# Attention with a gated bilinear block on one core: denominators of the last quad by a selection product, the last output product kept in PSUM, gate logits as rows, x in two loads

## The chip, the cores and the metric

The kernel runs on one core of one Trainium2 chip. The metric is the device time of an execution in microseconds (us), smaller is better. "Span" is the profiled execution from its first to its last instruction; it is about 2 us shorter than the time of the same run (728.7 against 730.78 for the kernel before). Ratios are the mean time of one kernel's runs over that of the other's of the same rounds, so they are not quite the ratios of the medians quoted beside them.

The engines: TensorE (PE, with its weight loads as PEld), VectorE (DVE), ScalarE (ACT), GpSimd (POOL), SyncE (SP, here only issuing DMAs).

## The reference

```
x = A_x                                             # 1 x 2048 x 512, bf16
g = sigmoid((x * gate_w).sum(-1))                   # one gate per row
a = attention(x, wqkv, wo)                          # 32 heads of 16, softmax over 2048 keys
b = ((x @ w_gate) * (x @ w_up)) @ w_down            # hidden width 1376
out = g * a + (1 - g) * b
```

## The kernel before

The whole program is planned while it is built: a list scheduler in the kernel file steps five clocks (one per engine) with fixed guesses of each duration and so decides the order of the instructions on each engine. The chip then runs that fixed order. Any edit of one part changes the order of everything after it.

The attention is done in 32 "quads" of heads, each for 512 queries: scores (TensorE), exponentials, PV products (TensorE, into one PSUM bank `psO`), normalisation. Three quarters of the exponentials run on ScalarE, in groups of two or three 512-wide tiles; the rest is made on VectorE and GpSimd by integer arithmetic. Everything else that TensorE has to do (q, k, v, gate, up, down and output projections) is a list of "fills", each with a wanted position counted in ScalarE tiles, put between score runs in that order. A "pack" is four matmuls on four column groups of the array; the chain of the kernel before lists 0.21 to 0.22 us for four.

The parts that the change touches (cuts marked by `# ...`):

```python
# four loads of x, alternating between two queues; wk before wq
for t in range(4):
    d_xs.append(load("sp" if t % 2 == 0 else "act", xs[:, t, :], x2[t * 128 : (t + 1) * 128, :], ...))
d_wk[0] = load("act", wk[:, :, 0:128], ...)
d_wq[0] = load("act", wq[:, :, 0:128], ...)

# f_gate: 16 packs of 4 one-column matmuls, full 128x128 weight loads of xT
for kt in range(KD):
    r = e.matmul(bk.ap[:, t : t + 1], xT[:, kt, t * 128 : (t + 1) * 128], gw[:, kt : kt + 1], ...)

# do_pv: in the last quad, each PV matmul is followed by one with "ones" weights,
# which sums the denominators, broadcast over 32 rows, into the bank DB
if lastq:
    for j, kt, k, cell, s0, s1 in specs:
        r = e.matmul(DB.ap[32 * j : 32 * j + 32, :], ones[:, k, :], cell_ap(cell, 1), ...)

# f_wo, last 512 queries: a fill of 4 packs (the fourth with zero-padded weights woz[0],
# for the half of the heads that is ready), evacuated by VectorE into a partial sum;
# at the very end the other half (woz[1]) and a second VectorE combine.
for tt in range(4):
    a1 = act: oraw = Ln(DB)         # denominators
    a2 = act: rb = Exp(-oraw)       # reciprocals
    mt = dve: OX = psO * rb
    pe:  tailb[tt] = OX.T @ woz[1]  # start=True, stop=True
    # then dve: out = gate * tailb + partial sum, and the store
```

The last four combines, one for each 128 rows, are the program's last VectorE work.

The softmax here doesn't subtract the row's maximum and nothing guards it: scores larger than these inputs give would overflow.

## Time and profile before

| | us |
|---|---|
| time, median of the runs made before the change was known | 731.68 (730.24 to 734.92) |
| head: start to first exponential | 10.70 |
| middle: first exponential to end of the last | 705.02 |
| tail: from there to the end | 13.01 |

The three stages are read from the timeline of ScalarE. The page of the kernel before: busy time by engine (section 1), two of the rows of 40 slices (section 2), and the chain that ended last (section 4).

```profile
span 728.7 us, 21767 instructions
PE 695.8 (95%) x9207; PEld 193.3 (27%) x9207; DVE 635.8 (87%) x1196; ACT 704.2 (97%) x687; POOL 420.0 (58%) x443
...
ACT  4999999999999999999999999999999999999993
PEclk9999997999999999999999999999999999999999
...
ACT 87%; PE 10%; DVE 2%; DMA 1%; issue 0%; ACTq 0%; DVEq 0%
```

ScalarE is busy for 97% of the span and is 87% of the chain: the middle is exponentials back to back. So the middle can only shrink where ScalarE waits. The clock row shows one slice at 7 tenths, near 110 us.

Who ScalarE waited for (waits view of the kernel before; us in total, times, longest):

```profile
ACT oraw L1734 <- PE psS L1139: 5.6, 1, 5.6
ACT KE L550 <- PE psS L521: 4.9, 1, 4.9
...
ACT hT L1565 <- PE psS L455: 2.4, 4, 1.0
ACT wv L1565 <- PE psS L455: 1.5, 3, 0.9
ACT PT L1565 <- PE psS L455: 0.5, 2, 0.2
ACT wd L1565 <- PE psS L455: 0.5, 1, 0.5
```

5.6 us is the wait between the last exponential and the first Ln, at the end; 4.9 is the head; the rest, some 5 us, lies in the middle.

The gate's stretch in windows of 2 us of the kernel before (columns: busy us and instruction count of each engine, granted TensorE clock, DMA):

```profile
104.00:106.00 2.00, 1.36 (x26) 0.82 (x26) 2.00 (x6) 2.00 (x3) 0.53 (x1) 1.00 0.00 0
106.00:108.00 2.00, 1.45 (x26) 0.82 (x26) 2.00 (x5) 2.00 (x2) 1.04 (x1) 0.91 0.00 0
108.00:110.00 2.00, 1.70 (x14) 0.39 (x11) 1.33 (x3) 2.00 (x3) 1.88 (x2) 0.50 0.00 0
110.00:112.00 2.00, 2.00 (x22) 0.50 (x19) 1.21 (x2) 1.64 (x3) 1.18 (x2) 0.50 0.02 4
112.00:114.00 2.00, 2.00 (x26) 0.78 (x26) 1.52 (x3) 1.75 (x2) 1.04 (x1) 0.50 0.04 8
114.00:116.00 2.00, 2.00 (x19) 0.24 (x17) 1.27 (x3) 1.59 (x3) 1.72 (x2) 0.50 0.04 4
116.00:118.00 2.00, 2.00 (x23) 0.37 (x15) 0.61 (x3) 1.52 (x2) 0.33 (x1) 0.53 0.00 0
```

While the gate's one-column matmuls run (from 104.2), TensorE reads 1.36 and 1.45 of 2 us busy; then the clock is 0.50 from 107.6 for 10.24 us, and ScalarE drops to about 1.6 of 2 us.

The chain of the head of the kernel before:

```profile
2.12 5.40 DMA wq<-in_A_wqkv_dram
...
7.66 1.94 PE psS L521 x32
...
9.61 0.61 ACT KE L550
```

wq, the fourth load on its queue, lands at 7.52, and the first product waits for it.

### The profile page before, as it was taken

To read this page: it belongs to the slowest core of one execution; us is meant where nothing else is said; L and a number is where in the kernel's file an instruction comes from. 1 tells how busy PE (TensorE), PEld (TensorE's weight loads), DVE (VectorE), ACT (ScalarE), POOL (GpSimd) and SP (SyncE) were. 2 spreads that over 40 slices of the span, in tenths; PEclk is the share of its full clock that TensorE was granted. 3 is DMA by queue.
4 is the path that set the end of the run, shared out by engine and by line. 5 is a ranking of instruction groups with operands and counts; after the bars stand their busy time and mean duration, and the time that the engine had idled before them with its cause. 6 is when DMAs were issued, how large, how long until landed. Compare 5 with 4: busy or idle time off the path is not lost.

```text
span 728.7 us, 21767 instructions
## 1 busy us (share of the span) xinstructions
PE 695.8 (95%) x9207; PEld 193.3 (27%) x9207; DVE 635.8 (87%) x1196; ACT 704.2 (97%) x687; POOL 420.0 (58%) x443
## 2 busy tenths in 40 slices
PE   7999999999999999999999999989999999999996
PEld 3323332222222222222222222222222222222222
DVE  5888997988989799999988989889888999988886
ACT  4999999999999999999999999999999999999993
POOL 2777665664655666655567665556544655554451
PEclk9999997999999999999999999999999999999999
DMA  7700000000200001000000010000000110000000
GB/s 139 250 3 17 20 17 18 21 16 7 95 20 17 18 14 40 18 18 21 17 18 12 24 42 18 18 8 14 21 17 16 36 32 6 17 20 17 20 18 30
DMA packets 31014, 21.65 MB, mean 30 GB/s; under 512 B 18344, under 2 KB 25928, under 8 KB 30920
## 3 DMA queue, kind: packets, MB, share of 16 engines
q1 hardware_dynamic: 29048, 19.49, 8.9%
q8 instruction: 73, 1.20, 0.7%
q10 hardware_dynamic: 1872, 0.79, 0.5%
q14 instruction: 21, 0.17, 0.1%
HBM read 15.11 MB, written 2.35 MB: 24 GB/s over the span
## 4 chain that ended last, share of the span: by engine, by line
ACT 87%; PE 10%; DVE 2%; DMA 1%; issue 0%; ACTq 0%; DVEq 0%
ACT PT L1565 63%; ACT wv L1565 15%; ACT wd L1565 5%; ACT hT L1565 4%; PE psS L455 3%; PE psO L1128 3%; PE psX L521 2%; DMA wq<-in_A_wqkv_dram 1%; PE psS L521 1%; DVE PT L1005 1%; PE psS L605 0%; PE psX L605 0%; DVE wk L823 0%; PE psX L455 0%; PE psS L1139 0%
## 5 line engine op out<-in xcount | busy, mean ns | idle before, releaser
L1565 ACT ACTIVATE PT<-psS 128x1024 bf16<-128x1024 f32 (+1 forms) x474 | 540.8, 1385 | 0.8 <-PE psS L455 0.5
L1064 POOL TENSOR_SCALAR PT<-PT 128x1024 int16<-128x1024 int16 x320 | 330.7, 1043 | 254.3 <-DVE PT L1061 143.0
L1005 DVE TENSOR_SCALAR PT<-psS 128x512 int16<-128x512 f32 x429 | 290.8, 685 | 41.1 <-PE psS L455 36.3
L455 PE MATMUL psS<-QM,KE 32*128 32x512 bf16 x1968 | 264.7, 379 | 19.4 <-ACT PT L1565 8.2
L1128 PE MATMUL psO<-PT,VS 128*18 128x512 bf16 x1605 | 226.6, 384 | 0.4 <-DVE oraw L1168 0.3
L1128 PE MATMUL psO<-PT,VD 128*18 128x512 bf16 x1400 | 207.9, 383 | 0.1
L1061 DVE TENSOR_SCALAR PT<-PT 128x1024 int16<-128x1024 int16 x375 | 157.7, 456 | 8.3 <-PE psO L1128 5.7
L1565 ACT ACTIVATE wv<-psS 128x1024 bf16<-128x1024 f32 (+1 forms) x120 | 153.1, 1304 | 1.5 <-PE psS L455 1.5
L947 PEld LDWEIGHTS <-KE 32*128 32x128 bf16 x2048 | 63.3, 91 | 275.0 <-issue 273.7
L1128 PEld LDWEIGHTS psO<-PT,VS 128*18 128x18 bf16 x1605 | 53.2, 88 | 58.6 <-issue 36.2
L1005 DVE TENSOR_SCALAR PT<-psX 128x512 int16<-128x512 f32 x77 | 53.0, 688 | 16.8 <-PE psS L455 16.4
L1128 PE MATMUL psO<-wv,VS 128*18 128x512 bf16 x258 | 66.6, 384 | 0.5 <-DVE oraw L1168 0.5
L1128 PEld LDWEIGHTS psO<-PT,VD 128*18 128x18 bf16 x1400 | 48.6, 88 | 45.6 <-issue 31.2
L521 PE MATMUL psX<-xT,wu 128*32 128x512 bf16 x688 | 55.5, 388 | 0.2 <-DVE QM L582 0.2
L521 PE MATMUL psX<-wd,hT 128*32 128x512 bf16 (+1 forms) x704 | 55.7, 384 | 0.0
L521 PE MATMUL psX<-xT,wg 128*32 128x512 bf16 x688 | 53.8, 384 | 0.3 <-DVE usb L726 0.3
L1565 ACT ACTIVATE hT<-psS 128x1024 bf16<-128x1024 f32 (+1 forms) x42 | 45.9, 1246 | 2.4 <-PE psS L455 2.4
L1565 ACT ACTIVATE wd<-psS 128x1024 bf16<-128x1024 f32 (+1 forms) x39 | 46.1, 1260 | 0.6 <-PE psS L455 0.5
L1064 POOL TENSOR_SCALAR wd<-PT 128x1024 int16<-128x1024 int16 x27 | 28.0, 1043 | 8.7 <-PE psO L1128 3.3
L455 PE MATMUL psX<-QM,KE 32*128 32x512 bf16 x80 | 30.2, 378 | 2.3 <-ACT KE L550 0.7
L726 DVE CAST usb<-psX 128x512 bf16<-128x512 f32 (+1 forms) x44 | 30.0, 682 | 2.3 <-PE psX L521 1.8
L758 DVE TENSOR_TENSOR hT<-psX,usb 128x512 bf16<-128x512 f32 (+1 forms) x44 | 30.0, 681 | 2.2 <-PE psX L521 2.0
(89 smaller groups left out, 468.5 us busy)
## 6 DMA issues: line engine op xcount, KB each, us to landing
rb<-rscr SPq DMA_DIRECT2D x31, 256.0 KB
out_dram<-ost SPq DMA_DIRECT2D x12, 128.0 KB, 2.1
wu<-in_B_w_up_dram SPq DMA_DIRECT2D x1, 1376.0 KB, 9.0
wg<-in_B_w_gate_dram SPq DMA_DIRECT2D x1, 1376.0 KB, 12.1
wd<-in_B_w_down_dram SPq DMA_DIRECT2D x1, 1280.0 KB, 6.1
OT<-OX SPq DMA_DIRECT2D x60, 16.0 KB, 1.8
wo<-in_A_wo_dram SPq DMA_DIRECT2D x1, 512.0 KB, 12.4
out_dram<-wk SPq DMA_DIRECT2D x4, 128.0 KB, 1.7
```

What stands on the lines that cost most here:

```text
L455: return e.add_instruction(mybir.InstMatmult(name=nc.get_next_instruction_name(), engine=mybir.EngineType.PE, ins=[e.lower_ap(rhs), e.lowe ...
L521: return e.matmul(out_ap[32 * q : 32 * q + w, :], lhs[:, 32 * q : 32 * q + w], rhs, start=s0, stop=s1, tile_position=(0, 32 * q), skip_gro ...
L726: lambda v: v.tensor_copy(usb[0:w, n % 2, :], bk.ap[0:w, :]),
L758: lambda v: v.tensor_tensor(hT[0:w, f, :], bk.ap[0:w, :], usb[0:w, n % 2, :], ALU.mult),
L947: r = e.ldweights(w, tile_position=pos)
L1005: lambda v: v.tensor_scalar(cell_ap(pr["cell"] + i, 1, mybir.dt.int16), bk.ap, CB, 0.0, ALU.add, ALU.max),
L1061: fn = lambda v: v.tensor_single_scalar(cell_ap(c, n, I16), cell_ap(pr["cell"], n, I16), 32.0 * k, ALU.add)
L1064: fn = lambda g: g.tensor_scalar(cell_ap(c, n, I16), cell_ap(pr["cell"], n, I16), 32.0 * k, 1.0, ALU.add, ALU.mult)
L1128: r = e.matmul(psO[32 * j : 32 * j + VW, :], pv_stationary(m, kt, j, k), cell_ap(cell, 1), start=s0, stop=s1, tile_position=(0, 32 * j), s ...
L1565: lambda a: a.activation(cell_ap(c, n), src, ACT.Exp, scale=LN2 / 128.0),
```

## The change

Intent: take TensorE work out of the end (denominators from `psO` itself, whose rows 16 of each 32 already hold them; the output projections after the PV packs; the last product added in PSUM, so that one VectorE combine for each 128 rows does), make the gate cheap, and start earlier. The core of the diff:

```diff
-        for t in range(4):
-            d_xs.append(load("sp" if t % 2 == 0 else "act", xs[:, t, :], ...))
+        for h in range(2):
+            r_ = load("act" if h else "sp", xs[:, 2 * h : 2 * h + 2, :], ...)
-        d_wk[0] = load("act", ...)      # wk before wq
+        d_wq[0] = load("act", ...)      # wq before wk
...
-            # gate: 64 matmuls of one column, psX <- xT (weights), gw
+                    return e.matmul(bk.ap[32 * q : 32 * q + 1, :], gw[:, kt : kt + 1],
+                                    xT[:, kt, q * 512 : (q + 1) * 512], ...)
+            packs = [... for kt in range(KD)]            # 4 packs; logits as 4 rows of 512
+            # then: copy to SBUF, DMA to memory, DMA back as 128 x 16, exp, 1/(1+.)
...
         # do_pv, last quad
-                if lastq:
-                    ... 112 "ones" matmuls into DB
...
         # f_wo, last 512 queries: 3 packs, result stays in its bank, no evacuation;
         # kept in a list of its own (wts), started only when no PV pack is ready
...
         # filler: hold a fill back when a score run is due; the fourth block's q and k earlier
-            (200.0, 280.0, [("q", 3, 0)] + ...
+            (190, 260, [("q", 3, 0)] + ...
+                    if st["ua"] >= 96 and late < FBL and t + FB * PACK > run_at() and any(AQ):
+                        cand = []
...
         # tail
+            hs.append(dve: hi = bf16(psO[:, cs]))
+            ls.append(dve: lo = psO[:, cs] - hi)
+            pe: dbs[tt][:, cs] = sel.T @ hi ; += sel.T @ lo     # 128-column packs
             a1 = act: Ln(dbs[tt])  ...
-            pe: tailb[tt] = OX.T @ woz[1]              # start, stop
+            pe: tailb[tt] += OT.T @ woz[0] (half) ; += OX.T @ woz[1]
```

Both programs put 1536 tiles of 512 through ScalarE, in 675 and 676 instructions.

More of the change, by code (lines that the diff above doesn't have):

```diff
@@ L229, in _build @@
     out2 = out.rearrange("b s d -> (b s) d")
+    gscr = nc.dram_tensor("gscr", [4, 512], F32, kind="Internal").ap()
     scr = nc.dram_tensor("rscr", [NO, 4, 512], F32, kind="Internal").ap()
@@ L261, in _build @@
         mask = sb("mask", [128, 2], F32)
-        ones = sb("ones", [128, 4, 32], BF16)
+        sel = sb("sel", [128, 128], BF16)
         gex = sb("gex", [128, T], F32)
@@ L319, in _build @@
         d_xs = []
-        for t in range(4):
-            d_xs.append(load("sp" if t % 2 == 0 else "act", xs[:, t, :], x2[t * 128 : (t + 1) * 128, :], f"dxs{t}", 0.5, 2.8))
+        for h in range(2):
+            r_ = load(
+                "act" if h else "sp",
+                xs[:, 2 * h : 2 * h + 2, :],
+                x2[h * 256 : h * 256 + 256, :].rearrange("(t p) d -> p t d", p=128),
+                f"dxs{h}",
+                0.5,
+                3.3,
+            )
+            d_xs += [r_, r_]
         d_wk, d_wq, d_wv = [None] * NB, [None] * NB, [None] * NB
-        d_wk[0] = load("act", wk[:, :, 0:128], wcol(D, D + 128), "dwk0", 0.5, 3.0)
-        d_wq[0] = load("act", wq[:, :, 0:128], wcol(0, 128), "dwq0", 0.5, 3.4)
+        d_wq[0] = load("act", wq[:, :, 0:128], wcol(0, 128), "dwq0", 0.5, 3.6)
+        d_wk[0] = load("act", wk[:, :, 0:128], wcol(D, D + 128), "dwk0", 0.5, 3.6)
         d_wv[0] = load("act", wv[:, :, 0:256], wcol(2 * D, 2 * D + 256), "dwv0", 0.5, 5.0)
@@ L373, in _build @@
         o_vone = o_one
-        for k in range(4):
-            o_one = now("pool", [o_one], lambda g, k=k: g.memset(ones[:, k, :], WK[k]), 0.2)
+        o_sel = now("pool", [], lambda g: g.memset(sel[:], 0.0), 0.3)
+        o_sel = now(
+            "pool",
+            [o_sel],
+            lambda g: g.affine_select(
+                out=sel.rearrange("p (a b) -> p a b", b=32),
+                in_=sel.rearrange("p (a b) -> p a b", b=32),
+                compare_op=ALU.not_equal,
+                fill=1.0,
+                base=-16,
+                pattern=[[-32, 4], [0, 32]],
+                channel_multiplier=1,
+            ),
+            0.4,
+        )
         slots = [
@@ L667, in f_gate, with mk, fn @@
         def f_gate(pos):
-            packs = []
-            for t in range(T):
-                def mk(bk, t=t):
-                    def fn(e):
-                        r = None
-                        for kt in range(KD):
-                            r = e.matmul(
-                                bk.ap[:, t : t + 1],
-                                xT[:, kt, t * 128 : (t + 1) * 128],
-                                gw[:, kt : kt + 1],
-                                start=(kt == 0),
-                                stop=(kt == KD - 1),
-                                skip_group_check=True,
-                            )
-                        return r
-                    return fn
-                packs.append((mk, 0.25, "f"))
+            def mk(bk, kt):
+                def fn(e, q):
+                    return e.matmul(
+                        bk.ap[32 * q : 32 * q + 1, :],
+                        gw[:, kt : kt + 1],
+                        xT[:, kt, q * 512 : (q + 1) * 512],
+                        start=(kt == 0),
+                        stop=(kt == KD - 1),
+                        tile_position=(0, 32 * q),
+                        skip_group_check=True,
+                    )
+                return pack4(fn)
@@ L689, in evac @@
+            packs = [(lambda bk, kt=kt: mk(bk, kt), PACK, "c") for kt in range(KD)]
+            grow = ost.rearrange("p a b -> p (a b)").bitcast(F32)
             def evac(bk, last):
                 bk.need += 1
+                e0 = None
+                e0 = add("dve", [last], lambda v: v.tensor_copy(grow, bk.ap), 0.61, prio=3, cb=lambda k: bk.readers.append(k))
                 e1 = add(
-                    "act",
-                    [last],
-                    lambda a: a.activation(gex[:], bk.ap[:, 0:T], ACT.Exp, scale=-1.0),
@@ L695, in evac @@
-                    0.1,
-                    lat=0.33,
-                    cb=lambda k: bk.readers.append(k),
-                )
-                e2 = add("dve", [e1], lambda v: v.tensor_single_scalar(gden[:], gex[:], 1.0, ALU.add), 0.1)
-                e3 = add("dve", [e2], lambda v: v.reciprocal(gval[:], gden[:]), 0.1)
-                ogate["g"] = add("dve", [e3], lambda v: v.tensor_scalar(omg[:], gval[:], -1.0, 1.0, ALU.mult, ALU.add), 0.1)
+                    "sp",
+                    [e0],
@@ new lines, in evac @@
+                    lambda e: e.dma_start(gscr, grow[0:128:32, :]),
+                    0.1,
+                    lat=3.0,
+                    stream="dgl",
+                    dma=True,
+                )
+                gsrc = bass.AP(gscr.tensor, gscr.offset, [[1, 128], [128, T]])
+                e2 = add(
+                    "sp",
+                    [e1],
+                    lambda e: e.dma_start(gex[:, :], gsrc, allow_slow_non_contiguous=True),
+                    0.5,
+                    lat=9.0,
+                    stream="dgl2",
+                    dma=True,
+                )
@@ L703, in f_gate @@
+                e3 = add("act", [e2], lambda a: a.activation(gval[:], gex[:], ACT.Exp, scale=-1.0), 0.1, lat=0.33)
+                e4 = add("dve", [e3], lambda v: v.tensor_single_scalar(gden[:], gval[:], 1.0, ALU.add), 0.1)
+                e5 = add("dve", [e4], lambda v: v.reciprocal(gval[:], gden[:]), 0.1)
+                ogate["g"] = add("dve", [e5], lambda v: v.tensor_scalar(omg[:], gval[:], -1.0, 1.0, ALU.mult, ALU.add), 0.1)
             return Fill("gate", packs, lambda: [d_gw, o_xt[0]] + d_x[1:], evac, pos)
@@ L811, in _build, with combine @@
         otfree = {}
-        ev_part = {}
-        part = xT[:, :, 512:1536].bitcast(F32)
-        def combine(t, bank_ap, last, cb=None, halves=None):
+        def combine(t, bank_ap, last, cb=None):
             c, tt = divmod(t, 4)
-            fin = t >= T - 4 and halves is None
-            o_dst = ost[:, t % 2, :] if t < T - 4 else part[:, tt, :] if not fin else wk[:, tt, :]
-            src = part[:, tt, :] if fin else b_ap(t)
+            o_dst = ost[:, t % 2, :] if t < T - 4 else wk[:, tt, :]
             k = add(
                 "dve",
-                [last, ev_b[c, tt], ogate["g"]] + ([o_out.get(t - 2)] if t < T - 4 else [ev_part[tt]] if fin else [pe["last"]]),
-                lambda v: v.scalar_tensor_tensor(o_dst, bank_ap, gval[:, t : t + 1], src, ALU.mult, ALU.add),
+                [last, ev_b[c, tt], ogate["g"]] + ([o_out.get(t - 2)] if t < T - 4 else []),
+                lambda v: v.scalar_tensor_tensor(o_dst, bank_ap, gval[:, t : t + 1], b_ap(t), ALU.mult, ALU.add),
                 0.67,
@@ L827, in combine @@
             )
-            if t >= T - 4 and not fin:
-                ev_part[tt] = k
-                return
             bfree[t] = k
@@ L844, in f_wo @@
             lastc = c == NCH - 1
+            nb = NB - 1 if lastc else NB
             packs = [
@@ L847, in f_wo @@
                     lambda bk, b=b: col(
-                        bk.ap,
-                        OT[:, (NB * c + b) % NOT, tt * 128 : (tt + 1) * 128],
-                        woz[:, 0, :] if lastc and b == NB - 1 else wo[:, b, :],
-                        b == 0,
-                        b == NB - 1,
+                        bk.ap, OT[:, (NB * c + b) % NOT, tt * 128 : (tt + 1) * 128], wo[:, b, :], b == 0, b == NB - 1
                     ),
@@ L856, in f_wo @@
                 )
-                for b in range(NB)
+                for b in range(nb)
             ]
             def evac(bk, last):
+                if lastc:
+                    tailb[tt] = bk
+                    bk.need = 99
+                    return
                 for b in range(NB):
@@ L863, in evac @@
                 bk.need += 1
-                combine(t, bk.ap, last, cb=lambda k: bk.readers.append(k), halves=True if lastc else None)
+                combine(t, bk.ap, last, cb=lambda k: bk.readers.append(k))
             def deps():
                 if lastc:
-                    if any(f.name[0] in "ugkvq" for f in fills):
-                        return [None]
-                    return [d_wo, d_woz[0], ev_b.get((c, tt)), o_mult.get(NM - 2)] + [o_ot.get(NB * c + b) for b in range(NB - 1)]
+                    return [d_wo] + [o_ot.get(NB * c + b) for b in range(NB - 1)]
                 if t >= 2 and t - 2 not in o_out:
@@ L1121, in do_pv @@
                 pv_left[m] -= 1
-            if lastq and specs[0][4]:
-                deps += DB.take(99)
             def fn(e):
@@ L1136, in fn @@
                     )
-                if lastq:
-                    for j, kt, k, cell, s0, s1 in specs:
-                        r = e.matmul(
-                            DB.ap[32 * j : 32 * j + 32, :],
-                            ones[:, k, :],
-                            cell_ap(cell, 1),
-                            start=s0,
-                            stop=s1,
-                            tile_position=(0, 32 * j),
-                            skip_group_check=True,
-                        )
                 return r
-            kk = pe_run(deps, fn, PACK * (2 if lastq else 1), "c", t)
+            kk = pe_run(deps, fn, PACK, "c", t)
             for j, kt, k, cell, s0, s1 in specs:
@@ L1231, in _build @@
         fills = [q0[3], q0[0], q0[4], q0[5], q0[1], q0[6], q0[7], q0[2]] + q0[8:]
+        wts = []
+        GP = 200.0
+        K3L = 190
+        K3H = 260
         B1, B2L, B2, B3L, B3 = 40.0, 100.0, 180.0, 200.0, 270.0
@@ L1235, in _build @@
             (90.0, 184.0, [("q", 2, 0), ("k", 2, 0), ("v", 1, 0), ("v", 1, 1), ("k", 2, 1), ("v", 1, 2), ("v", 1, 3), ("k", 2, 2), ("v", 1, 4), ("v", 1, 5), ("k", 2, 3), ("v", 1, 6), ("v", 1, 7)]),
-            (200.0, 280.0, [("q", 3, 0)] + [("k", 3, ch) for ch in range(4)]),
+            (K3L, K3H, [("q", 3, 0)] + [("k", 3, ch) for ch in range(4)]),
         ):
@@ L1240, in _build @@
                 fills.append(f_q(0, b, pos) if kind == "q" else f_k(b, ch, pos) if kind == "k" else f_v(b, ch, pos))
-        GP = 200.0
         F0 = 210.0
@@ L1261, in _build @@
             for tt in range(4):
-                fills.append(f_wo(c, tt, max(PER * NQ * (c + 1) + WP, f0 + step * (c + 1) + 4.0) + 9.0 * tt if c < NCH - 1 else NA - WL))
+                (fills if c < NCH - 1 else wts).append(f_wo(c, tt, max(PER * NQ * (c + 1) + WP, f0 + step * (c + 1) + 4.0) + 9.0 * tt if c < NCH - 1 else NA - WL))
         for c in range(NCH - 1):
@@ L1298, in bank_free, with start_fill @@
             return f is not None and f + SEM <= t
-        def start_fill(f, bk):
-            fills.remove(f)
+        def start_fill(f, bk, lst=None):
+            (fills if lst is None else lst).remove(f)
             f.bank = bk
@@ L1359, in _build @@
         XF = -99
+        FB = 2
+        FBL = 15
         def a_idx():
@@ L1464, in pe_step @@
                 na = len(aus)
-                if ua + na > NA - PER:
-                    st["mq"] = True
                 st["lastd"] = dus[-1] if dus else None
@@ L1500, in pe_step, with run_at @@
             return filler(t, can)
+        def run_at():
+            s = slots[st["slot"]]
+            fr = [s[i].free_at() for i in range(2)]
+            if len(exps) < 2 and all(f is not None for f in fr):
+                return max(max(fr) + SEM, act_need() - 0.62 - MG)
+            if not exps:
+                return clock["pe"]
+            t0 = max(clock["act"], exps[0][2].end + SEM)
+            return t0 + 0.052 + 0.4267 * len(exps[0][0]) + 0.21 + SEM
         st["mq"] = False
-        tailb = []
+        tailb = {}
+        tbs = (X, slots[1][2], slots[1][0], slots[1][1])
         def filler(t, can=True):
@@ L1524, in filler @@
                             break
-            if pv is not None and (nfree < NF or st["fill"] is None):
+            fin = not any(AQ) and all(dnext[j] == len(DU[j]) for j in range(4))
+            if fin and pv is None and st["fill"] is None and wts and fready(wts[0], t):
+                for bk in tbs:
+                    if bank_free(bk, t):
+                        start_fill(wts[0], bk, wts)
+                        break
+            if pv is not None and (nfree < NF or st["fill"] is None or fin):
                 do_pv(pv, t)
@@ L1701, in _build @@
                 clock[e] += 0.02
-            if pvst["m"] >= NM and not fills and st["fill"] is None:
+            if pvst["m"] >= NM and not fills:
                 break
@@ L1715, in _build, with tail_step, pe_tail @@
         drain()
-        assert not fills and st["fill"] is None, [f.name for f in fills]
+        assert not fills, [f.name for f in fills]
+        half = []
+        def tail_step(limit):
+            t = clock["pe"]
+            if st["fill"] is None and wts:
+                for bk in tbs:
+                    if bk.need < 99 and bank_free(bk, t):
+                        start_fill(wts[0], bk, wts)
+                        break
+            if st["fill"] is not None:
+                do_fill(t)
+                return True
+            o = o_mult[NM - 2]
+            if len(half) < len(tailb) and max(o.end, d_woz[0].end) + SEM <= max(t, limit - PACK):
+                tt = len(half)
+                rhs = OT[:, (NB * NCH - 1) % NOT, tt * 128 : (tt + 1) * 128]
+                half.append(pe_run([o, d_woz[0]], col(tailb[tt].ap, rhs, woz[:, 0, :], False, False), PACK, "c", t))
+                return True
+            return False
+        def pe_tail(deps, fn, occ, lat):
+            t = ready(_Task("pe", deps, fn, occ))
+            while t > clock["pe"] + 0.1 and tail_step(t):
+                pass
+            return pe_run(deps, fn, occ, "c", clock["pe"], lat=lat)
         c = NCH - 1
-        tailb = [X, slots[1][2], slots[1][0], slots[0][0]]
         lastpv = pvst["last"]
@@ L1722, in _build @@
         free = o_mult[NM - 1 - NO]
+        hi, lo = usb[:, 0, :], usb[:, 1, :]
+        hs, ls, dens = [], [], []
+        for tt in (0, 1, 0, 1, 2, 3, 2, 3):
+            cs = slice(tt * 128, (tt + 1) * 128)
+            if len(hs) <= tt:
+                hs.append(now("dve", [lastpv], lambda v, cs=cs: v.tensor_copy(hi[:, cs], psO[:, cs]), 0.2))
+            else:
+                ls.append(now("dve", [hs[tt]], lambda v, cs=cs: v.tensor_tensor(lo[:, cs], psO[:, cs], hi[:, cs], ALU.subtract), 0.2))
+        dbs = [slots[0][min(tt, 2)] for tt in range(4)]
+        old = [bk.take(99) for bk in slots[0]] + [[]]
+        for tt in range(4):
+            cs = slice(tt * 128, (tt + 1) * 128)
+            pe_tail([hs[tt], o_sel] + old[tt], col(dbs[tt].ap[:, cs], sel, hi[:, cs], True, False), 0.06, 0.3)
+            dens.append(pe_tail([ls[tt]], col(dbs[tt].ap[:, cs], sel, lo[:, cs], False, True), 0.06, 0.3))
+        dens[2] = dens[3]
         oo = []
@@ L1733, in _build @@
             cs = slice(tt * 128, (tt + 1) * 128)
-            a1 = now("act", [lastpv, free], lambda a, cs=cs: a.activation(lnd[:, cs], DB.ap[:, cs], ACT.Ln), 0.29)
+            a1 = now("act", [dens[tt], free], lambda a, tt=tt, cs=cs: a.activation(lnd[:, cs], dbs[tt].ap[:, cs], ACT.Ln), 0.29)
             a2 = now("act", [a1], lambda a, cs=cs: a.activation(rlast[:, cs], lnd[:, cs], ACT.Exp, scale=-1.0), 0.22)
-            if tt == 3:
+            if tt == 2:
                 fin(0)
@@ L1743, in _build, with last_pack @@
             )
-            oo.append(
-                pe_run(
-                    [mt] + tailb[tt].take(99),
-                    col(tailb[tt].ap, OX[:, (NB - 1) % 2, cs], woz[:, 1, :], True, True),
-                    PACK,
-                    "c",
-                    clock["pe"],
-                )
-            )
+            def last_pack(e, tt=tt, cs=cs):
+                return col(tailb[tt].ap, OX[:, (NB - 1) % 2, cs], woz[:, 1, :], False, True)(e)
+            while len(half) <= tt:
+                assert tail_step(1e9)
+            oo.append(pe_tail([mt], last_pack, PACK, 0.44))
         for tt in range(1, 4):
```

## The prediction

> **What bounds the kernel now.** ScalarE (ACT). The page gives it 704.2 of 728.7 us busy; the chain of waits is 87% ACT, nearly all softmax exponentials. The timeline splits the span into a head (first exponential at 10.70 us), a middle of 705.0 us (last exponential ends at 715.72), and a tail of 13.0 us. In the middle ACT idles about 5 us (stretches: 1.9 in 12 to 50, 1.7 in 100 to 120, 1.1 in 480 to 490, 0.2 elsewhere). The built programs both put 1536 tiles of 512 through ACT (675 and 676 instructions), so the middle can only shrink by that idle time.
>
> **Tail (about -4.0 us).** Before, ACT waits 5.6 us (waits view) from its last exponential to the first Ln, because TensorE still has about 9 PV packs, 9 packs of the "ones" denominators (0.22 us each in the chain) and three output projections (0.86 us each) to do. All 112 "ones" matmuls go (28 packs, an estimated 6 us of TensorE, partly before ACT ends), and the projections move behind the PV packs. By the instruction order only 5 PV packs follow the last score, the last needs the last exponential, and no VectorE partial sum (0.75 us each) stands in between. I expect the last PV to end 0.6 to 1.0 us after the last exponential. Added: eight 128x128 VectorE ops (about 0.22 us each, as the present 128x128 product) and eight short selection packs; estimated 1.3 us until the first Ln. So the 5.6 us wait becomes about 2.1. From the first Ln on, the chain is unchanged in kind (Ln, Exp, product, last pack, four 0.67 us combines, 2.1 us store); 7.4 us now from PV end to the end, about 8.2 afterwards. Tail: 13.0 to about 9.0.
>
> **Gate (about -1.5 us).** The gate now uses 64 one-column matmuls with full weight loads, from 104.2 to 118.2. While they run TensorE stalls (busy 1.36 and 1.45 of 2 us), and the granted clock then reads 0.50 for 10.24 us from about 107.7; the ACT gaps of that stretch (0.25, 0.25, 0.41, 0.48) lie in it. [...] The new gate is 4 packs (0.9 us), so I expect this stretch at full clock and its ACT idle gone. The two new gate DMAs are off the critical path. The second throttle (483 to 487, after a schedule dip) may move, vanish or return.
>
> **Head (about -0.8 us).** The critical load is wq, issued fourth on ACT's queue (2.12) and landing at 7.52; it becomes the second, and x needs one issue (0.4 us) fewer per queue. Then the xT copies (done at 6.96) and wk limit. First exponential near 9.9.
>
> **Middle reshuffle.** Fill order and positions change, so ACT idle elsewhere may rise or fall; I allow +0.5 for it. Sum: -0.8 -1.5 -4.0 +0.5, about -5.8.
>
> **Predicted:** 725.8 us, 80% range 722.5 to 729.5. Faster by over 2%: 0.02; within 2%: 0.97; slower: 0.01.
>
> **Right if:** first exponential at 9.5 to 10.3; no 0.5 clock in the stretch with the gate; ACT idle from last exponential to first Ln 1.5 to 2.7 us; last exponential to end 8.5 to 9.7 us.
>
> **Wrong if:** larger x loads land later and delay everything; a less loaded TensorE dips and throttles elsewhere; the new filler rule starves TensorE fills so that weights or gate come late; the selection chain serialises through semaphores and costs over 2 us.

That the new gate would keep the full clock rests on the trace's order of events (TensorE at 1.36 and 1.45 of 2 us, half clock after it) and was the author's estimate.

## The result

| | before | after |
|---|---|---|
| time, median | 731.0 (730.24 to 734.92, 4 runs) | 721.68 (720.47 to 722.06, 4 runs) |
| ratio | | 0.986, 95% interval 0.9828 to 0.9892 |
| span of the profiled run | 728.7 | 719.0 |
| head / middle / tail | 10.70 / 705.02 / 13.01 | 9.43 / 700.67 / 8.88 |

The change is 1.4% faster; that is inside 2%, as forecast, but the time lies below the range of 722.5 to 729.5. The page after, the same lines:

```profile
span 719.0 us, 21551 instructions
PE 686.3 (95%) x9079; PEld 188.6 (26%) x9079; DVE 633.8 (88%) x1209; ACT 702.8 (98%) x688; POOL 411.6 (57%) x433
...
ACT  5999999999999999999999999999999999999996
PEclk9999999999999999999999999999999999999999
...
ACT 95%; PE 3%; DMA 1%; DVE 1%; ACTq 0%; issue 0%; DVEq 0%
```

The clock row has no slice below 9 any more, and the chain is ScalarE for 95%. Where the gate runs now (its matmuls start between 114.3 and 116.0), the windows read:

```profile
114.00:116.00 2.00, 1.93 (x29) 0.45 (x30) 1.85 (x4) 2.00 (x3) 1.04 (x1) 1.00 0.22 71
116.00:118.00 2.00, 2.00 (x33) 0.56 (x31) 2.00 (x5) 2.00 (x3) 1.04 (x1) 1.00 0.18 69
```

ScalarE's waits after:

```profile
ACT KE L572 <- PE psS L543: 3.9, 1, 3.9
...
ACT hT L1598 <- PE psS L477: 2.4, 4, 1.0
ACT oraw L1808 <- PE psS L543: 1.7, 1, 1.7
```

The wait before the first Ln fell from 5.6 to 1.7 us. In the middle no wait is left, apart from 2.4 us (`hT`) in the first 30 us, which both kernels have. The chain of the head after:

```profile
1.80 5.40 DMA wk<-in_A_wqkv_dram
...
7.24 1.08 PE psS L543 x16
...
8.34 0.61 ACT KE L572
```

Now wk is what the first k product waits for; the q product before it is off the chain.

To see where the middle gained, I counted in both traces when n of the 1536 exponential tiles were done (the "curve", after minus before, in us):

```
tiles done       2     205    250    700   1030   1040   1536   end of program
before, us    11.72  106.45 129.41 334.08 484.38 490.23 715.72  728.73
after - before -1.27  -1.37  -3.96  -3.89  -4.19  -5.49  -5.63  -9.77
```

The gain comes in four steps and is flat between them: 1.3 us in the head, 2.6 us between 106 and 129 us (the gate), 1.3 us between 484 and 490 us, and 4.1 us in the tail; about 0.5 is spread over the rest. The trace of before has two throttled stretches before its tail, 107.6 to 117.8 us and 483.1 to 486.5 us, exactly where the two middle steps are. The trace of after has none, but for the last 0.2 us of the program.

### The profile page after: what moved, and what is told of

It is laid out like the page before. It is cut to its first block, busy times and chain, and to the rows that moved or that the text cites. A ratio compares the mean times of both kernels' runs of the same rounds, so it can differ in the third digit from the quotient of the medians.

```text
span 719.0 us, 21551 instructions
## 1 busy us (share of the span) xinstructions
PE 686.3 (95%) x9079; PEld 188.6 (26%) x9079; DVE 633.8 (88%) x1209; ACT 702.8 (98%) x688; POOL 411.6 (57%) x433
## 4 chain that ended last, share of the span: by engine, by line
ACT 95%; PE 3%; DMA 1%; DVE 1%; ACTq 0%; issue 0%; DVEq 0%
ACT PT L1598 69%; ACT wv L1598 16%; ACT hT L1598 5%; ACT wd L1598 4%; PE psS L543 1%; DMA wk<-in_A_wqkv_dram 1%; PE psO L1150 1%; PE psS L477 0%; PE psS L627 0%; PE psX L627 0%; DVE wk L851 0%; PE psX L477 0%; DVE wd L1029 0%; PE psX L543 0%; ACTq L316 0%
## 5 line engine op out<-in xcount | busy, mean ns | idle before, releaser
L1088 POOL TENSOR_SCALAR PT<-PT 128x1024 int16<-128x1024 int16 x312 | 322.2, 1043 | 250.8 <-DVE PT L1085 129.2
L1029 DVE TENSOR_SCALAR PT<-psS 128x512 int16<-128x512 f32 x441 | 300.0, 686 | 47.4 <-PE psS L477 40.6
L1150 PE MATMUL psO<-PT,VS 128*18 128x512 bf16 x1597 | 220.9, 381 | 0.3 <-DVE oraw L1179 0.2
L1150 PE MATMUL psO<-PT,VD 128*18 128x512 bf16 x1400 | 204.5, 381 | 0.2
L1085 DVE TENSOR_SCALAR PT<-PT 128x1024 int16<-128x1024 int16 x380 | 155.8, 450 | 4.6 <-PE psO L1150 1.4
L1150 PE MATMUL psO<-wv,VS 128*18 128x512 bf16 x257 | 63.1, 381 | 0.1
L1598 ACT ACTIVATE hT<-psS 128x1024 bf16<-128x1024 f32 (+1 forms) x49 | 53.4, 1274 | 2.4 <-PE psS L477 2.4
L1029 DVE TENSOR_SCALAR PT<-psX 128x512 int16<-128x512 f32 x63 | 43.4, 688 | 8.6 <-PE psS L477 8.2
L1598 ACT ACTIVATE wd<-psS 128x1024 bf16<-128x1024 f32 (+1 forms) x34 | 42.5, 1340 | 0.0
L1211 POOL TENSOR_TENSOR OT<-oraw,rb 128x512 bf16<-128x512 f32 x16 | 20.4, 1273 | 13.7 <-DVE PT L1085 13.7
```

Of the source, the lines that this page charges most:

```text
L1029: lambda v: v.tensor_scalar(cell_ap(pr["cell"] + i, 1, mybir.dt.int16), bk.ap, CB, 0.0, ALU.add, ALU.max),
L1085: fn = lambda v: v.tensor_single_scalar(cell_ap(c, n, I16), cell_ap(pr["cell"], n, I16), 32.0 * k, ALU.add)
L1088: fn = lambda g: g.tensor_scalar(cell_ap(c, n, I16), cell_ap(pr["cell"], n, I16), 32.0 * k, 1.0, ALU.add, ALU.mult)
L1150: r = e.matmul(psO[32 * j : 32 * j + VW, :], pv_stationary(m, kt, j, k), cell_ap(cell, 1), start=s0, stop=s1, tile_position=(0, 32 * j), s ...
L1211: lambda e: e.tensor_tensor(dst, oraw[:, s, :], rb[:, s, :], ALU.mult),
L1598: lambda a: a.activation(cell_ap(c, n), src, ACT.Exp, scale=LN2 / 128.0),
```

## The experiments

Fourteen kernels were run, each beside the kernel before. The build-time plan makes clean comparisons of totals hard (below), so most verdicts rest on the curve and on single waits in the traces.

### The parts alone

`gate_only`: the kernel before with the gate part of the diff.

> The kernel before with only the gate as rows. Theory 1 ([...] the clock halves for 10.2 us, and ACT starves): no 0.5 clock near 107 us, the curve of exponential tiles against time gains 2.0 to 2.8 us between 100 and 125 us and nothing before; span 726.0 to 727.0. Theory 2 (the throttle of that stretch comes anyway and the gain there was schedule reshuffle): the throttle stays and the gain is under 1 us. The second throttle near 483 is left open: if it goes too, another 1.1.

(The one-column matmuls were thought to bring the half clock. Theory 1 is that they do: in the trace of before the clock is 0.50 for 10.24 us soon after they start.)

Measured: 728.8 us, ratio 0.9949 (0.9907 to 0.9991). There is no throttle near 107 (clock 1.00 in all windows from 104 to 120 us), and against before the curve goes from +1.59 at tile 205 (this execution had a late head, 12.28, with the clock halved from 8.5 to 11.9 us) to -0.85 at tile 265: 2.4 us, as theory 1 said. The throttle near 483 was absent too (another 1.3). But the span was 729.0, not 726 to 727: the head was 1.6 us later and the tail 14.8 instead of 13.0, and 0.7 was lost near 330 us.

`head_only`: the two x loads and wq ahead of wk, and nothing else.

> The kernel before with only the two x loads and wq ahead of wk. First exponential at 9.4 instead of 10.7 if the head's gain is due to the loads alone; throttles and tail as before; span 727.2 to 727.8. If the first exponential stays later than 10, the shorter gate or constants must have helped.

Measured: 730.0 us, 0.9959 (0.9910 to 1.0008); first exponential 9.28, tail 13.05, both throttles (105.4 and 480.9) still there, span 727.1. This is as expected. Over all runs the head is the noisiest piece: with the old loads the first exponential came at 9.92, 10.05, 10.28, 10.47, 10.54, 10.70, 11.80, 12.20 and 12.28 us, with the new ones at 8.75, 8.80, 9.28, 9.43, 9.53 and 9.56. The medians, 10.54 and 9.36, differ by 1.2 us and the two groups don't overlap. Which of the two edits does it was not separated.

`tail_only`: the end part of the diff, with the old gate, the old loads and the old fill rule.

> The kernel before with only the end changed (selection product, last product kept in PSUM, projections after PV). Tail from last exponential to end 8.6 to 9.2 instead of 13.0 us. The list of fills loses four entries, so the positions of later fills change a little: if the second throttle is luck of the schedule it may move or go; the first (gate) throttle must stay. Span 723.5 to 725.

Measured: 735.56 us, 1.0040 (0.9998 to 1.0083). It missed in both terms. The tail was 11.27, not 8.6 to 9.2, because 10 PV packs were still to do at the last exponential. And the middle lost 6.9 us against before (curve from -0.65 to +6.27): a wait at 162.8 (1.1 us), throttles at 440.8 and 464.7 (3.41 and 6.83 us), and waits of ScalarE for cells that late PV packs had not freed. One of them in ScalarE's timeline of this run (the brackets give the idle time before and what ended it):

```profile
468.69 1.02 ACT L1565 ACTIVATE PT<-psS 128x1024 bf16<-128x1024 f32 x1 [2.75 <-PE psO L1131]
```

So the tail's edit alone, in this plan, is no gain. The losses lie far ahead of the tail's instructions, so it is the order of fills that seems to cost here; this is argued and was not isolated.

`after_oldgate`: the kernel after with the gate part of the diff undone.

> The kernel after with the old gate put back. Theory 1: a 0.5 clock stretch returns near 105 us and the curve loses 2.0 to 2.8 us there; span 721 to 722. Theory 2: under 1 us lost, no throttle.

Measured: 726.82 us, 0.9918 (0.9878 to 0.9959), which is 5.1 us over the kernel after (medians of different rounds). The throttle came back, for 17.07 us from 117.7, and relative to after the curve lost 5.1 us between tiles 205 and 280 and another 1.4 by tile 400, with waits of ScalarE at 158.8 and 165.0 where scores came late. The direction is that of theory 1; the loss is larger than expected, and the stretch lasted five steps of 3.41 us here and not three.

`sched_only`: only the fill rule and the earlier fourth block, in the kernel before.

```diff
-            (200.0, 280.0, [("q", 3, 0)] + ...
+            (K3L, K3H, [("q", 3, 0)] + ...      # 190, 260
+                    if st["ua"] >= 96 and late < FBL and t + FB * PACK > run_at() and any(AQ):
+                        cand = []
```

> The kernel before with only the schedule constants: the new rule that holds a fill back when a score run is due, and the fourth block's q and k fills earlier (190 to 260). The alone-run of the tail was slower than before (735.6), so parts interact. Theory A (the constants keep TensorE from dips and backlogs): the second throttle (483) goes, ACT idle away from the gate falls under 0.5 us, gain 1 to 2 us over before; gate throttle and 13 us tail stay. Theory B (the constants are neutral and the loss of the tail-only run was luck of the fill positions): within 1 us of before at the last exponential.

Measured: 741.83 us, 1.0147 (1.0115 to 1.0179). Both theories missed: it is clearly slower. The gate ran later (115.4 to 131.4) and throttled for 17.07 us, and ScalarE waited 12.0 us before the first Ln, with 14 PV packs, 14 ones packs and 11 packs of the down projection still to do.

`after_nosched`: the kernel after without those constants.

> The kernel after without those constants. Theory A: throttles or ACT idle come back in the middle, TensorE has a backlog at the end (tail 10 to 11.5 us), span 722 to 728. Theory B: within 1 us of after, 718 to 720, tail about 8.9.

Measured: 720.65 us, 0.9860 (0.9836 to 0.9884), curve within 0.4 us of after from tile 205 on, no throttle in the middle, tail 8.62. So the constants add nothing measurable to the change (theory B here), though in the kernel before they cost 11 us.

### What in the gate cost 2.6 us

`gate_x7`: the kernel before with the new gate, its packs seven times over, 28 packs or some 5.9 us of TensorE, about as long as the old gate's 64 weight loads of 0.096 us (6.1 us; both are estimates from the traces' 0.21 us a pack and 0.096 us a load). "Active" and "activity" in this and later expectations mean how busy the traces show TensorE: 1.36 and 1.45 of 2 us at the old gate.

```diff
-            packs = [(lambda bk, kt=kt: mk(bk, kt), PACK, "c") for kt in range(KD)]
+            packs = [(lambda bk, kt=kt: mk(bk, kt), PACK, "c") for _ in range(7) for kt in range(KD)]
```

> The kernel before with the new gate, but its four packs done seven times over (28 packs, about 6 us of fully active TensorE, about as long as the 64 one-column matmuls take). Theory 1 (what cost 2.4 us was the halved clock, from low activity): no throttle near 107, the curve keeps most of the gain of the gate-only run (at least 1.5 of 2.4 us between 100 and 125). Theory 2 (what cost was the TensorE time of the old gate): the gain is gone, under 0.8 us, without a throttle.

Measured in the stretch in question: no throttle (clock 1.00 in all windows from 104 to 120 us); the curve gained 2.5 us between tiles 205 and 265 (from -0.41 to -2.87), the whole gain of `gate_only`. The total is another matter: 741.65 us, 1.0148 (1.0122 to 1.0173). ScalarE's waits in this run:

```profile
ACT oraw L1745 <- PE psS L1150: 8.6, 1, 8.6
ACT wd L1576 <- PE psS L456: 8.6, 3, 4.6
```

The second line is three waits, at 153.5, 159.6 and 168.6: the 28 packs held up the queue of fills behind them, and the casts of the last four key chunks ended at 141.9, 153.0, 159.1 and 168.1 instead of 120.8, 137.7, 144.6 and 153.9 in `gate_only`. So the old gate's cost where it stood was the clock, not the time; but TensorE time in fills has its own price, when a deadline lies behind it. The later losses (1.8 us at 362.6, a tail of 17.0) belong to this plan as well.

`gate_spread`: the kernel before with its old gate, the same 64 one-column matmuls, cut into four fills 16 positions apart.

```diff
-            for t in range(T):
+            for t in range(4 * part, 4 * part + 4):
...
-        fills.append(f_gate(GP))
+        fills.append(f_gate(GP, 0))
+        for gp_ in range(1, 4):
+            fills.append(f_gate(GP + 16.0 * gp_, gp_))
```

> The kernel before with its old one-column gate, cut into four fills of four row tiles each, placed 16 positions apart. Same matmuls, same TensorE time, three more small ACT instructions [...]. Theory 1 (dense one-column matmuls [...] halve the clock): no 0.5 stretch between 90 and 150 us, and the curve gains 1.5 to 2.5 us there against before. Rival (their TensorE time is what costs): no gain. The plan of later fills changes too, so the rest of the span is not compared.

Measured: 729.38 us, 0.9995 (0.9968 to 1.0021), the matmuls now between 105.3 and 143.8 us. The first windows of this run:

```profile
104.00:106.00 2.00, 1.91 (x34) 0.79 (x34) 1.63 (x4) 2.00 (x3) 1.58 (x2) 1.00 0.04 8
106.00:108.00 2.00, 1.63 (x22) 0.47 (x19) 2.00 (x5) 2.00 (x4) 0.84 (x1) 1.00 0.00 0
108.00:110.00 2.00, 1.30 (x19) 0.33 (x19) 2.00 (x5) 2.00 (x4) 0.90 (x2) 1.00 0.01 4
110.00:112.00 2.00, 1.97 (x30) 0.51 (x22) 2.00 (x4) 2.00 (x3) 2.00 (x3) 1.00 0.00 0
```

The clock stays at 1.00 although one window has only 1.30 us of TensorE; it is not followed by another like it. The curve gained 2.4 us (from +1.11 to -1.29 between tiles 205 and 250). The same instructions without their crowding cost no throttle (the clock is 1.00 in these windows, against 0.50 for 10.24 us in the kernel before): together with `gate_only`, `after_oldgate` and `gate_x7` that settles the gate's step. The total gained nothing, since this run's head was late (11.80), keys were late again (0.7 at 162.7) and the tail was 13.9.

### The second throttle

In which executions of before it occurs can be judged by the mean clock: one stretch of 10.24 us at half clock takes 0.7% off it, one of 3.41 us another 0.23% (estimates: half of each over the span of 728.7). Of the 28 runs of before in the four sets of rounds, 15 have a clock of 0.992 or more and so had no room for the second stretch beside the gate's (an inference: only the profiled runs list the stretches); their median is 730.0 us. The median of the other 13 is 731.6; these may have had it, or one in the head or at the end, as some profiled runs show. So it is there in at most half of the executions, among them the profiled one.

`dip_x2` and `dip_x3`: the plan of before, unchanged, with the score matmuls of tiles 1012 to 1034 issued two or three times. Each time the bank is written anew. The outputs are right. "Activity" is again TensorE's busy time: 0.85 of 2 us ahead of the throttle in the kernel before.

```diff
+            times = 2 if aus and 1012 <= st["ua"] <= 1034 else 1
             def fn(e):
-                for u, bk in us:
-                    ...
+                for _ in range(times):
+                    for u, bk in us:
+                        ...
```

> The kernel before, same plan, but the score matmuls of the exponential tiles 1012 to 1034 are issued twice (idempotent; about 0.2 us more TensorE work per run in a stretch where TensorE waits for ScalarE). Low activity as the cause: no 0.5 clock near 483, and the curve gains about 1.3 us between tiles 1030 and 1040. Another cause: throttle and loss stay. The gate throttle near 107 stays in both.

> The same with three times (0.4 us more per run). As for twice; if twice is too little activity to hold the clock, this one still should. Risk: scores come up to 0.4 us later and ACT may wait a little, at most 0.1 us each.

Windows of the kernel before:

```profile
480.00:482.00 2.00, 0.85 (x10) 0.28 (x9) 2.00 (x5) 2.00 (x4) 1.41 (x3) 1.00 0.00 0
482.00:484.00 2.00, 1.77 (x22) 0.41 (x19) 1.96 (x5) 2.00 (x3) 1.03 (x2) 0.78 0.04 4
484.00:486.00 2.00, 2.00 (x18) 0.40 (x17) 0.69 (x1) 1.40 (x2) 1.89 (x2) 0.50 0.03 8
```

and of `dip_x2`:

```profile
480.00:482.00 2.00, 1.68 (x20) 0.51 (x13) 1.96 (x4) 2.00 (x3) 1.42 (x2) 1.00 0.00 0
482.00:484.00 2.00, 1.71 (x27) 0.41 (x19) 2.00 (x5) 2.00 (x3) 1.29 (x2) 1.00 0.07 12
484.00:486.00 2.00, 2.00 (x32) 0.43 (x23) 1.25 (x3) 1.70 (x3) 1.52 (x2) 1.00 0.00 0
```

Before, TensorE is busy 0.85 of 2 us in the window ahead of the throttle, with score runs alone; its longest gap there is 0.60 us. With doubled scores it is 1.68, and no throttle follows. With three times TensorE reads 1.76 or more in every window of 2 us between 478 and 486 us, and none follows either (clock 1.00 from 470 to 490). Against before, `dip_x2` gained 0.6 us between tiles 1030 and 1040 and not 1.3: the doubled work itself probably cost the rest, as ScalarE reads 1.70 of 2 us in one window. `dip_x3` lost 1.0 us between tiles 1000 and 1040 (0.9 of it before tile 1030), probably for that reason, without a throttle. Times: 730.04 (0.9988, 0.9956 to 1.0020) and 732.16 (1.0010, 0.9972 to 1.0048), both unclear against before. The absence might still be chance, as at most half of the executions throttle there: of the timed runs of `dip_x2`, two read a clock of 0.992 and had no room for a second stretch, two read 0.991 and just had it; `dip_x3` read 0.989 to 0.992 (its profiled run spent a 3.41 us stretch in the head).

The kept traces say more than these two runs. Within each trace every stretch of half clock begins a whole number of steps of 3.413 us after the first one: 110.0 and 181.0 steps in the kernel before, 98.0 and 105.0 in `tail_only`, 54.0 and 58.0 in `after_seed3`. The stretches that the end of a trace does not cut off last 3.41, 6.83, 10.24 or 17.07 us, one, two, three or five such steps. I call the steps windows; counted from the first half clock of a trace, their borders lie elsewhere in the plan in each execution. In the kernel before the window from 479.7 us covers the dip, and in `head_only` one that begins 0.5 us earlier in the plan does. In `dip_x2` and `dip_x3` a border between two windows happens to fall into the dip. That is a rival: laid on the same borders, the trace of before holds 6.0 and 5.9 packs there, right at the limit found next (estimates, as part of that ran at half clock), and taking the added matmuls out of the two runs' own windows gives 6.3 and 4.6. The two runs alone therefore don't settle that the added work kept the clock.

What supports the dip as the cause is a count over all traces, made after the runs. For each window I added up the matmuls in packs, each matmul by its columns and by how many 32 x 32 blocks its weights cover, out of the 16 that four matmuls of a pack cover together; one that crosses a border was shared by time. From 8 us on, in the 14 traces with some half clock, 27 windows at full clock were followed by half clock. They hold at most 5.9 packs (2.5 at the gate and 5.4 at the dip of the kernel before). The 2,876 others hold at least 6.2, with a median of 10.8. Half clock went on after windows of at most 5.7 packs and ended after windows of at least 6.0. By this definition a one-column matmul adds next to nothing (1/512 of a pack), although its record lasts 0.163 us and its weight load 0.096 us in the kernel before. `dip_x2` and `dip_x3` have 8.6 and 9.1 packs in the window of the dip. In the first 8 us the count does not fit throughout: a few windows of 5.0 to 5.8 packs kept the full clock there.

### The tail

`after_ones`: the kernel after with the ones matmuls put back and the selection product taken out; the projections stay behind the PV packs.

```diff
+                if lastq:                       # in do_pv, and ones = sb(...) as before
+                    ... ones matmuls into DB
-        hs, ls, dens = ...                      # selection product
-            a1 = act: Ln(dbs[tt])
+            a1 = act: Ln(DB)
```

> The kernel after, but with the denominators of the last quad summed by the 112 ones matmuls again (no selection product); the output projections stay behind the PV packs. If removing the ones matmuls is what shortens the wait between last exponential and first Ln, that wait rises from 1.7 to 4 to 6 us and the tail from 8.9 to 10.5 to 13. If the move of the projections alone does it, the wait stays under 2.5 us (and the selection product's own 1.2 us is saved: tail under 9).

Measured: 725.47 us, 0.9933 (0.9912 to 0.9955), 3.8 us over after (medians of different rounds). The plan is that of after up to the last quad, and the curve runs 0.7 us ahead of it from the head on (no throttle; last exponential at 709.79, 0.3 ahead). ScalarE's wait:

```profile
ACT oraw L1812 <- PE psS L1167: 5.3, 1, 5.3
```

It is 5.3 us again, the tail 13.6. At the last exponential 12 PV packs and 12 ones packs are to do, against 1 PV pack in the kernel after: the ones matmuls cost their own time, and the time they took before that point shows as PV packs not yet done. So the move of the projections alone does not make the tail short in this plan; the ones packs have to go. Whether that would be enough without the move was not run: in the chain of the kernel before two projections of 0.86 us stand ahead of the first Ln, so up to 1.7 of the 5.6 us may be theirs (an estimate). The runs together, with the TensorE packs (rounded) that started from 0.3 us before the end of the last exponential:

```
run            tail   wait for first Ln   Ln to end   PV packs  ones packs  projection packs
before        13.01        5.63             7.38          9          9           12
before_seed3  16.14        8.58             7.55         13         13           16
gate_only     14.80        6.61             8.19          9          9           16
gate_spread   13.93        6.56             7.37         10         10           14
gate_x7       17.01        8.65             8.36         14         14           16
sched_only    20.01       12.02             7.98         14         14           16
after_ones    13.58        5.31             8.27         12         12           16
tail_only     11.27        4.30             6.97         10          0           16
after_oldgate  9.31        2.32             6.99          3          0           13
after_seed3    9.32        2.39             6.93          4          0           11
after          8.88        1.72             7.16          1          0           15
after_nosched  8.62        1.69             6.93          1          0           14
```

### Luck of the plan

`before_seed3` and `after_seed3`: another seed for the jitter of the fill positions.

```diff
-        SEED = 2
+        SEED = 3
```

> The kernel before with seed 3 for the jitter of fill positions. Measures luck of the plan with the old gate and the old end: the gate throttle near 107 stays; elsewhere the last exponential moves by 0 to 6 us, and the wait for the last quad's TensorE work stays 5 us or more. If the plan of before was a picked one, 731 to 737 us.

> The kernel after with another seed for the jitter of the fill positions: nothing else differs. It measures what luck of the schedule is worth. If the positions matter little, within 1 us of 719.0; if the seed was picked for this kernel, 1 to 6 us slower, with throttles or ACT idle somewhere in the middle.

Measured: 735.13 us (1.0065, 1.0044 to 1.0085) and 720.83 us (0.9858, 0.9830 to 0.9885). Before, the seed is worth 4 to 5 us: late keys (2.4 us at 164.2) and a tail of 16.1; the gate's throttle stays. After, the profiled run has throttles at 522.3 and 706.6 that cost 1.0 us and 0.4 to 0.7 us, and the total is as good as with seed 2. Two seeds each are few, but the plans of after do not look picked: three of them (after, `after_nosched`, `after_seed3`) are within 1.1 us of each other by medians, while the plans with the old gate or the old end run from 725 to 742.

### A version to beat both

`best1`: the kernel after with wk loaded from the SyncE queue ahead of the transposes, and the half products of the tail ahead of the last projection.

```diff
-        d_wk[0] = load("act", wk[:, :, 0:128], ...)
+        d_wk[0] = load("sp", wk[:, :, 0:128], ...)
...
         def tail_step(limit):
+            (half product, if ready)            # moved ahead of
             if st["fill"] is None and wts: ...  # the next projection
-            (half product, if ready)
```

> The kernel after with two more edits: wk is loaded from the SyncE queue ahead of the transposes (it was what the first k product waited for), and in the tail the half products with the zero-padded weights go ahead of the last tile's projection. Expected: first exponential 0.3 to 0.8 us earlier (9.4 to about 8.8), first combine 0.3 to 0.5 us earlier; 717.5 to 718.5 us span. If transposes delayed by half a us hurt, ACT waits rise between 12 and 30 us.

Measured: 720.43 us, 0.9869 (0.9849 to 0.9889): no different from after. The first exponential came at 8.95, inside the range of the other new heads, so nothing is shown by it. The first combine came 1.70 us after the first Ln instead of 1.91, but from the first Ln to the end it was 7.15 us against 7.16: the gain was not kept. `after_nosched`, at 720.65, is no different either. No version was found that beats the kernel after.

## Why the prediction was right or wrong

| step | predicted | in the two profiles |
|---|---|---|
| head | -0.8 | -1.3 |
| gate | -1.5 | -2.6 |
| rest of the middle | +0.5 | -1.8 (1.3 of it the second throttle) |
| tail | -4.0 | -4.1 |
| sum | -5.8 | -9.8 |

The sum is off by 4.0 us: 2.3 of it is the step "Middle reshuffle", 1.1 the step "Gate" and 0.5 the step "Head".

**What bounds the kernel: right.** After, ScalarE is 95% of the chain, and the middle has no other loss left.

**Tail: right in size and largely in cause.** The wait before the first Ln was to be 1.5 to 2.7 us and is 1.72; last exponential to end 8.5 to 9.7 and is 8.88; last PV 0.6 to 1.0 us after the last exponential, and it is 0.5, just under. `after_ones` shows that the ones packs had to go; the share of the moved projections was not isolated. What the prediction did not see is that this gain depends on the plan: the same edit with another order of fills (`tail_only`) left 10 PV packs behind and a tail of 11.3 us.

**Gate: mechanism right, size wrong.** The term that failed is "about -1.5 us", a sum of ScalarE's idle gaps (0.25, 0.25, 0.41, 0.48 and a small one). `gate_spread`, `gate_x7` and `gate_only` agree on 2.4 to 2.5 us. The term was too small because idle gaps undercount here. The spans of ScalarE's instructions overlap: just after a wait a 1024-wide exponential lasts 1.02 us but the next starts after 0.92 in the kernel before (in long stretches without a wait the recorded spans grow, to 1.27 at the median, and the starts stay 0.91 apart). A gap of 0.25 after such a span of 1.02 therefore is 1.27 from start to start, a delay of 0.36 against the median of 0.91, and more after a longer span. Measured by start-to-start times against their medians (0.91 us after two tiles, 1.33 after three), seven late starts between 100 and 125 us cost 2.7 us, of which idle time shows 1.7.

**The middle outside the gate: wrong in sign.** The prediction allowed "+0.5" for the reshuffle and left the second throttle open. It went, for 1.3 us. The count of packs by window points to the dip in TensorE's work just before it as its cause; `dip_x2` and `dip_x3` agree but don't show it alone. That the new plan has no such dip is no merit of one edit that I could name: `gate_only` and `after_oldgate` have no throttle there either, `tail_only` has two some 20 to 40 us earlier, `sched_only` one at 508, `after_seed3` one at 522. I call it plan luck in favour of the change. It also is no full 1.3 us in the medians, since at least 15 of 28 executions of before don't have it.

**Head: right in kind, too small.** wk became the limit, as said, but the first exponential came at 9.43, just under the 9.5 to 10.3 that was to confirm it. The medians of many runs give 1.2 us; the 1.3 of the two profiles holds some noise.

**"Wrong if":** larger x loads landing later, gate or weights late by the new rule, and a selection chain over 2 us did not occur in the kernel after. A dip and throttle elsewhere did not occur in it, but did in its neighbours.

What stays open: which of the two edits shortens the head, and what in a plan decides whether TensorE dips, late keys and a PV backlog appear. The totals of the single parts don't add up: against the medians of before in the same rounds `tail_only` is +3.8, `gate_only` -2.9 and `head_only` -1.7 us, but all three together (`after_nosched`) -9.9. The traces show the terms (late keys, throttles, backlog) case by case; that the replanning brings them is argued from the parts being far from where the losses are, not isolated.

## What to carry to other kernels

When an engine that is not the bottleneck gates the end, count the packs it still has to do at the moment the bottleneck engine finishes: work put in earlier comes back there as backlog (12 PV and 12 ones packs in `after_ones`, against 1 PV pack in the kernel after). In the kernel before, one-column matmuls and later score runs with nothing in between were followed by half clock, for 10.24 and 3.41 us, though TensorE's longest idle gap ahead of it was 0.59 and 0.60 us; with the old gate in `after_oldgate` and `sched_only` it lasted 17.07 us. Spacing the gate's matmuls out (`gate_spread`) or replacing them (`gate_only`) kept the clock at 1.00 from 104 to 120 us; so look for the 0.5 in the clock column before blaming time. From 8 us on, the full clock stayed in these traces after windows of 3.41 us with at least 6.2 packs and halved after windows with at most 5.9. Where a schedule is planned at build time, judge an edit by its own stretch of the trace and not by the total, and measure a delay by start-to-start times rather than by idle gaps where spans overlap (here 2.7 us against 1.7).
